# Row counts that are multiples of 16, and each expert's rows requested before the weight piece instead of behind it

## The chip, the cores and the metric

One Trainium2 chip, one of its cores. The metric is device time in microseconds (us) of one execution, lower is better. PE is the matrix engine, DVE the vector engine, ACT the scalar engine, POOL the GpSimd engine, SP the sync engine, which in this kernel only issues DMA transfers.

## The reference, cut to what matters

Three stages follow each other. A linear recurrence over 768 steps (4 batches, 8 heads, head size 48) gives 3072 rows of 384 numbers. A mixture of experts then picks one of 8 experts for each row; last comes a dense feed-forward layer. Only the middle stage is touched by the change:

```python
def _moe_ref(x, w_gate, w1, w2):          # x: 3072 x 384, w1: 8 x 384 x 1024, w2: 8 x 1024 x 384
    logits = x @ w_gate
    expert_idx = np.argmax(logits, axis=1)
    ...                                    # gate_w: the softmax probability of the chosen expert
    for e in range(E):
        mask = expert_idx == e
        xe = x[mask]
        h = np.maximum(xe @ w1[e], 0.0)
        ye = h @ w2[e]
        out[mask] = gate_w[mask, None] * ye

def _moe2_ref(x, w_in, w_out):            # 384 -> 2048 -> 384
    h = x @ w_in
    g = np.maximum(0.01 * h, h)
    return g @ w_out
```

## The kernel before, in words

**Stages.** Until about 150 us the kernel computes the recurrence, chooses an expert for each token and scatters the rows by expert into a DRAM table `xs` (8 regions; a row is 386 floats, 1544 bytes: 384 values, the gate weight, the token's number). From about 140 to 380 us the experts run, one after the other, sorted by how many tokens they got. From about 377 us to the end the dense layer runs over blocks of 512 tokens.

**Places and windows.** The experts stand in eight places; place k has room for `CAPS[k]` rows, fixed when the kernel is built, and the matmuls always run over the whole room. Place 0 is cut in two (256 and 224 rows), so there are nine windows, numbered 0 to 8; window i from 1 on serves place i - 1. Each window has eight steps f = 0 to 7, and n = 8 i + f counts all of them. A step issues `first(n)` (9 matmuls of 128 hidden units, tile `ph`; three products each, since every number is split into a high and a low part), then ACT and DVE make the hidden tile `hh` of it (L891, L892), and two steps later `second` uses it (9 matmuls, tile `y`, L911).

**Rows of a window.** `load_rows(i)` (L847) brings the rows of a window from `xs` into the tile `erows` with one DMA: the rows are cut into nj slices of w = cap / nj, slice after slice side by side on w partitions, so that the transfer runs over w partitions, then over nj rows on each. There is a single `erows` buffer. `turn(i)` (L863 to L867) transposes the rows on PE, one third of the columns at a time, in steps f = 2, 4 and 6 of the window before (5, 6 and 7 in window 1); ACT and DVE copy the result into `xe`. So `load_rows(i + 1)`, issued at f = 0 of window i, needs only that `turn(i)` has finished, which it did at f = 6 of the window before.

**Weights.** An expert's weights come in eight pieces of 384 KB. `piece_load(n + 2)` (L764) is issued by SP in step n into one of three `raw` buffers; it waits until `piece_split(n - 1)` is done: ACT copies the high half (L777), and for odd pieces POOL, for even ones DVE, makes the low half (L785). Pieces split in window i are used in window i + 1.

**Conversion.** In parallel `convert` turns the weights of the last layer from 64-bit numbers into 32-bit ones: SP loads `raw64` (L795), ACT makes `size` (L805), DVE does six operations (L815 to L835), and SP stores to `w2f` (L837).

**Orders.** Every engine runs its instructions in the order written, and so does SP's queue of transfers. At f = 0 of window i, with n = 8 i, SP's order before the change is: `piece_load(n + 2)`, then `load_rows(i + 1)`, then the `raw64` load and the `w2f` store. The loop that fixes this is `experts`:

```python
        for n, (i, f) in enumerate(seq):
            if n + AHEAD >= nf:
                self.piece_load(n + AHEAD)
            if n >= nf:
                if f == 0 and i + 1 < len(WINDOWS):
                    self.load_rows(i + 1, xs)
...
            if n >= nf:
                self.piece_split(n)
            self.convert_step(n, pools)
```

Of the kernel before, what the change touches and what calls it, by code (L numbers as in the profile page):

```python
# [21 lines left out]
P = 128  # L22
# [42 lines left out]
LISTS = 4  # L65
OUT_AT = (0, 1, 3, 5, 7, 9, 11, 13)

CAPS = (480, 456, 432, 416, 400, 392, 384, 372)
EARLY = 256
WINDOWS = [(0, 0, EARLY), (0, EARLY, CAPS[0] - EARLY)] + [(k, 0, CAPS[k]) for k in range(1, 8)]  # L70
PAD = 260
assert sum(CAPS) <= S * B + PAD

# [12 lines left out]
class Kernel:  # L86
# [110 lines left out]
    def cap_table(self):  # L197
        for k in range(E):
            self.nc.vector.memset(self.caps[:, k : k + 1], float(CAPS[k]))

# [114 lines left out]
    def load_start(self, k):  # L315
        SP, ACT = mybir.EngineType.SP, mybir.EngineType.Activation
        self.starts.append(self.index(self.starts_i[0:1, k : k + 1], NT + PAD - CAPS[k], [ACT, SP]))

# [27 lines left out]
    def attention(self, xs, clist, extra, first_weights, const, route):  # L346
        nc, tc, a = self.nc, self.tc, self.a
        with ExitStack() as ctx:
# [64 lines left out]
            def zero_region(e):  # L413

                n = max(CAPS) - SURE
                nc.sync.dma_start(
# [421 lines left out]
            del self.conv[i]  # L838


    def load_rows(self, i, xs, eng=None):

        k, off, cap = WINDOWS[i]
        nj = -(-cap // P)
        w = cap // nj
        self.win[i] = t = self.rowpool.tile([P, 4, RW], F32, tag="rows", name="erows")
        (eng or self.nc.sync).dma_start(  # L847
            out=t[:w, :nj, :],
            in_=xs[bass.ds(self.ids[k] * NT + off, cap), :].rearrange("(j p) c -> p j c", p=w),
        )  # L850

    def turn(self, i, ps, tag, cs=range(KD)):
        nc = self.nc
        k, off, cap = WINDOWS[i]
        nj = -(-cap // P)
        w = cap // nj
        for c in cs:
            if c == 0:
                self.xT[i] = self.xpool.tile([P, 2, KD, 512], F32R, tag="x", name="xe")
            x = self.xT[i]  # L860
            pt = ps.tile([P, 512], F32, tag=tag, name="pt") if ps else tag[c]
            for j in range(nj):
                nc.tensor.transpose(  # L863
                    pt[:, j * w : (j + 1) * w], self.win[i][:w, j, c * P : (c + 1) * P], self.ident[:w, :w]
                )
            nc.scalar.activation(out=x[:, 0, c, :cap], in_=pt[:, :cap], func=AF.Copy)
            nc.vector.tensor_tensor(  # L867
                out=x[:, 1, c, :cap], in0=pt[:, :cap], in1=x[:, 0, c, :cap].bitcast(F32), op=ALU.subtract
            )

    def list_rows(self, k, xs, clist):
        at = self.starts[k]
        self.nc.sync.dma_start(
            out=clist[bass.ds(at, CAPS[k]), :] if k else clist[0 : CAPS[0], :],
            in_=xs[bass.ds(self.ids[k] * NT, CAPS[k]), DM : DM + 2],
# [53 lines left out]
    def experts(self, xs, clist, pools, meanwhile):  # L929
        nf = FF // P  # L930
        seq = [(i, f) for i in range(len(WINDOWS)) for f in range(nf)]
        rest = iter(seq)

        self.starts = [0]

        self.sums(0, pools)

        def second(count):
            for _ in range(count):
                self.second(*next(rest), pools)  # L940

        for n, (i, f) in enumerate(seq):
            if n + AHEAD >= nf:
                self.piece_load(n + AHEAD)
            if n >= nf:
                if f == 0 and i + 1 < len(WINDOWS):
                    self.load_rows(i + 1, xs)
                if f == 6:
                    for k in {1: (1,), 2: (2, 3), 3: (4, 5), 4: (6, 7)}.get(i, ()):
                        self.load_start(k)  # L950

                if i >= 2 and f % LISTS == 1 and (n - 2 * nf) // LISTS < E:
                    self.list_rows((n - 2 * nf) // LISTS, xs, clist)
# [3 lines that stand above are left out]
            if n == nf:  # L957
                second(1)
            if n == 2 * nf:
                second(1)  # L960
            self.first(i, f, pools)
            meanwhile(n)

            second(2 if n == nf - 1 else 0 if nf <= n <= nf + 1 or n == 2 * nf else n >= LAG)
            if n == nf - 1:
                self.turn(1, pools["ps"], "h")

            turns = (5, 6, 7) if i == 1 else (2, 4, 6)
            if n >= nf and f in turns:
                if i + 1 < len(WINDOWS):  # L970
                    self.turn(i + 1, pools["ps"], "h", [turns.index(f)])
                else:
                    self.split_x(0, turns.index(f))
        self.rest = second
# [428 lines left out]
```

## Time and profile before

| | us |
|---|---|
| median of 3 runs | 795.03 (794.87 to 795.36) |
| the profiled execution | 792.69 |
| its span, first to last instruction | 791.1 |

In the profiled execution PE was busy 755.4 us of the span (95%), DVE 469.9, ACT 376.8, POOL 191.3; the mean granted clock of PE was 0.977 of full speed. The row of an instruction gives its start, how long it took, engine and line, tiles and shape; neighbours of one kind are merged (x9 is nine). A busy PE can be waiting inside its pipeline, so a stretch is better read from the starts of the groups than from the busy share.

### The profile page before, as it was taken

Reading aid. Unit: us, or ns where it says so; the run is one execution under the profiler, and the core shown is the slowest. Engines: PE = TensorE matmul, PEld = TensorE weight load, DVE = VectorE, ACT = ScalarE, POOL = GpSimd, SP = SyncE. Lnnn points to the kernel's source line nnn. Section 1 sums busy time; section 2 is a strip of 40 time slices with the busy share of each in tenths; the row PEclk is TensorE's granted clock in tenths of the full one; section 3 lists DMA queues with packets and bytes.
Section 4 is the critical chain, followed back from the end, with each engine's and each line's share of the span. In section 5 each row is a group of like instructions: output and inputs, shape, how many; then the busy total and the mean of one; then the engine's idle time right before and its main releaser. Section 6 shows DMA issues by size and latency. Waiting matters only on the chain.

```text
span 791.1 us, 13214 instructions
## 1 busy us (share of the span) xinstructions
PE 755.4 (95%) x4908; PEld 696.2 (88%) x4908; DVE 469.9 (59%) x837; ACT 376.8 (48%) x801; POOL 191.3 (24%) x214
## 2 busy tenths in 40 slices
PE   6999988999999999799999999999999999999994
PEld 3889977899999999799999899999999999999993
DVE  6878876568888999599874443433433343343331
ACT  5989976255555545355444423332342243233331
POOL 5768883402222232123100200020020001002001
PEclk8989999999999999899999999999999999999998
DMA  8899875468757757757530000010010001001001
GB/s 230 255 270 276 264 235 171 157 184 247 214 169 241 236 193 228 188 177 226 136 113 15 11 30 1 1 41 0 1 41 1 1 0 41 1 1 40 1 1 44
DMA packets 52373, 92.62 MB, mean 117 GB/s; under 512 B 12789, under 2 KB 30762, under 8 KB 52298
## 3 DMA queue, kind: packets, MB, share of 16 engines
q1 hardware_dynamic: 49017, 81.47, 34.8%
q0 software_dynamic: 3280, 10.21, 3.5%
q8 instruction: 40, 0.66, 0.4%
q14 instruction: 36, 0.29, 0.1%
HBM read 73.11 MB, written 18.57 MB: 116 GB/s over the span
## 4 chain that ended last, share of the span: by engine, by line
PE 66%; issue 8%; DMA 2%; DVE 2%; POOL 1%; ACT 0%; SPq 0%; POOLq 0%; ACTq 0%
PE ph L1005 21%; PE o L1024 21%; PE ph L886 12%; PE y L911 11%; DMA erows<-xs 2%; PE pt L863 1%; POOL out L1037 1%; DVE t L832 1%; POOL xs L742 0%; ACT z L1036 0%; DVE c L785 0%; POOL c L785 0%; DVE hh L892 0%; DVE t L823 0%; DVE t L829 0%
## 5 line engine op out<-in xcount | busy, mean ns | idle before, releaser
L1024 PE MATMUL o<-c,gg 128*128 128x384 f32 x1152 | 215.5, 336 | 0.0
L1005 PE MATMUL ph<-x,c 128*128 128x512 f32 x864 | 213.9, 392 | 0.0
L1024 PEld LDWEIGHTS o<-c,gg 128*128 128x128 f32 x1152 | 202.1, 188 | 8.2 <-DVE gg L1014 0.2
L1005 PEld LDWEIGHTS ph<-x,c 128*128 128x128 f32 x864 | 161.2, 188 | 28.5
L1011 DVE TENSOR_TENSOR s<-s,ph 128x512 f32<-128x512 f32 x96 | 65.9, 686 | 165.4 <-ACT s L1010 165.4
L1010 ACT ACTIVATE s<-ph 128x512 f32<-128x512 f32 x96 | 57.3, 597 | 174.0 <-PE ph L1005 165.0
L886 PE MATMUL ph<-xe,c 128*128 128x256 f32 (+8 forms) x648 | 126.8, 343 | 2.5 <-DVE xe L867 2.5
L911 PE MATMUL y<-hh,c 128*128 128x256 f32 (+8 forms) x648 | 122.0, 333 | 0.0
L886 PEld LDWEIGHTS ph<-xe,c 128*128 128x128 f32 x648 | 111.8, 196 | 4.6 <-DVE xe L867 2.6
L785 POOL TENSOR_TENSOR c<-raw,c 128x768 fp32r<-128x768 f32 x32 | 60.2, 1881 | 221.5 <-ACT c L777 150.5
L911 PEld LDWEIGHTS y<-hh,c 128*128 128x128 f32 x648 | 110.0, 190 | 2.1
L1014 DVE TENSOR_TENSOR gg<-s,gg 128x512 fp32r<-128x512 f32 x96 | 66.4, 692 | 67.0 <-ACT gg L1013 66.3
L1037 POOL DMA_INDIRECT out<-z,to x24 | 24.2, 1009 | 320.9 <-ACT z L1036 302.3
L1013 ACT ACTIVATE gg<-s 128x512 fp32r<-128x512 f32 x96 | 60.7, 632 | 81.2 <-DVE s L1011 81.2
L777 ACT ACTIVATE c<-raw 128x768 fp32r<-128x768 f32 x80 | 67.1, 840 | 3.6 <-DMA raw<-in_wE 2.9
L891 ACT ACTIVATE hh<-ph 128x256 fp32r<-128x256 f32 (+8 forms) x72 | 34.5, 479 | 71.2 <-PE ph L886 68.8
L471 ACT ACTIVATE A<-ident,av 128x128 f32<-128x128 f32 x192 | 58.6, 392 | 0.3 <-DVE av L461 0.2
L785 DVE TENSOR_TENSOR c<-raw,c 128x768 fp32r<-128x768 f32 x48 | 45.6, 951 | 11.3 <-ACT c L777 10.7
L832 DVE SCALAR_TENSOR_TENSOR t<-raw,t 128x384 f32<-128x384 uint32 x32 | 45.6, 1425 | 1.1
L892 DVE SCALAR_TENSOR_TENSOR hh<-ph,hh 128x256 fp32r<-128x256 f32 (+8 forms) x72 | 38.5, 535 | 8.3 <-ACT hh L891 8.3
L482 PE MATMUL pa<-R,K 48*128 48x128 f32 x384 | 29.7, 297 | 7.1 <-DVE A L488 5.3
L488 DVE COPY_PREDICATED A<-strict,pa 128x1024 f32<-128x1024 int32 x24 | 32.4, 1351 | 3.9 <-PE py L518 2.6
(175 smaller groups left out, 668.8 us busy)
## 6 DMA issues: line engine op xcount, KB each, us to landing
raw<-in_wE SPq DMA_DIRECT2D x64, 384.0 KB
raw<-in_w2nd SPq DMA_DIRECT2D x32, 384.0 KB
w2f<-t SPq DMA_DIRECT2D x32, 192.0 KB
raw<-w2f SPq DMA_DIRECT2D x16, 384.0 KB
k<-in_k SPq DMA_DIRECT2D x24, 192.0 KB
r<-in_r SPq DMA_DIRECT2D x24, 192.0 KB
v<-in_v SPq DMA_DIRECT2D x24, 192.0 KB
kT<-in_kT SPq DMA_DIRECT2D x40, 96.0 KB
```

What stands on the lines that cost most here:

```text
L471: nc.scalar.activation(out=d["A"][:, h % 2, h // 2, :], in_=self.ident, func=AF.Copy, scale=d["av"][:, h : h + 1],)
L777: self.nc.scalar.activation(out=w[:, 0, c], in_=t, func=AF.Copy)
L785: eng.tensor_tensor(out=w[:, 1, c], in0=t, in1=w[:, 0, c].bitcast(F32), op=ALU.subtract)
L832: nc.vector.scalar_tensor_tensor(out=x, in0=low.bitcast(U32), scalar=2.0**-52, in1=x, op0=ALU.mult, op1=ALU.mult)
L886: nc.tensor.matmul(ph[:, :cap], w[:, wl, c * 512 + o : c * 512 + o + P], self.xT[i][:, xl, c, :cap], start=(c == 0 and n == 0), stop=(c == ...
L911: nc.tensor.matmul(self.y[i][m][:, :cap], w[:, wl, o : o + P], t[:, xl, :cap], start=(f == 0 and n == 0), stop=(f == FF // P - 1 and n == 2),)
L1005: nc.tensor.matmul(ph, w[:, wl, c * 512 + off : c * 512 + off + P], x2[b][:, xl, c, :], start=(c == 0 and i == 0), stop=(c == KD - 1 and i ...
L1010: nc.scalar.activation(out=s, in_=ph, func=AF.Copy, scale=0.01)
L1011: nc.vector.tensor_tensor(out=s, in0=s, in1=ph, op=ALU.max)
L1013: nc.scalar.activation(out=t[:, 0, :], in_=s, func=AF.Copy)
L1014: nc.vector.tensor_tensor(out=t[:, 1, :], in0=s, in1=t[:, 0, :].bitcast(F32), op=ALU.subtract)
L1024: nc.tensor.matmul(o[b][k][:, :DM], t[:, gl, k * P : (k + 1) * P], w[:, wl, (f % 4) * DM : (f % 4 + 1) * DM], start=(f == 0 and i == 0), s ...
```

## The change

Two things. The rooms of places 1, 5 and 7 go from 456, 392 and 372 rows to 448, 400 and 368, so that each room is a multiple of 16; as 368 isn't divisible by 3, a new function `window` takes the smallest number of slices that divides the room (368 is four slices of 92 instead of 372 as three of 124). And from window 2 on `load_rows(i + 1)` is issued at the head of step f = 0, before `piece_load(n + 2)`; in window 1 it stays behind it.

```diff
-CAPS = (480, 456, 432, 416, 400, 392, 384, 372)
+CAPS = (480, 448, 432, 416, 400, 400, 384, 368)
...
+    def window(self, i):
+
+        k, off, cap = WINDOWS[i]
+        nj = next(n for n in range(-(-cap // P), 5) if cap % n == 0)
+        return k, off, cap, nj, cap // nj
+
     def load_rows(self, i, xs, eng=None):
 
-        k, off, cap = WINDOWS[i]
-        nj = -(-cap // P)
-        w = cap // nj
+        k, off, cap, nj, w = self.window(i)
...
     def turn(self, i, ps, tag, cs=range(KD)):
         nc = self.nc
-        k, off, cap = WINDOWS[i]
-        nj = -(-cap // P)
-        w = cap // nj
+        k, off, cap, nj, w = self.window(i)
...
         for n, (i, f) in enumerate(seq):
+
+            if i > 1 and f == 0 and i + 1 < len(WINDOWS):
+                self.load_rows(i + 1, xs)
             if n + AHEAD >= nf:
                 self.piece_load(n + AHEAD)
             if n >= nf:
-                if f == 0 and i + 1 < len(WINDOWS):
+                if i == 1 and f == 0:
                     self.load_rows(i + 1, xs)
```

## Rows read from the trace of the kernel before

**Rows 1.** Who waited for whom, engine PE, whole span: total, times, longest.

```profile
PE pt L863 <- DMA erows<-xs: 7.6, 2, 5.5
```

**Rows 2.** PE in order of time, windows 6 to 8.

```profile
315.78 0.49 PE L863 MATMUL pt<-ident,erows 128*128 128x128 f32 x3
...
327.30 1.74 PE L911 MATMUL y<-hh,c 128*128 128x384 f32 x9
334.54 0.88 PE L863 MATMUL pt<-ident,erows 124*128 124x124 f32 x3 [5.50 <-DMA erows<-xs]
...
339.58 1.75 PE L886 MATMUL ph<-xe,c 128*128 128x384 f32 x9
341.17 1.73 PE L911 MATMUL y<-hh,c 128*128 128x384 f32 x9
342.74 0.48 PE L863 MATMUL pt<-ident,erows 124*128 124x124 f32 x3
...
346.24 1.75 PE L886 MATMUL ph<-xe,c 128*128 128x384 f32 x9
...
360.62 1.69 PE L911 MATMUL y<-hh,c 128*128 128x372 f32 x9
```

**Rows 3.** The chain that ended last, 300 to 340 us: start, us, what.

```profile
317.70 1.83 POOL c L785
319.55 0.34 SPq L764
...
320.13 14.36 DMA erows<-xs
```

**Rows 4.** Stretches: length, busy PE, PEld, DVE, ACT, POOL; PE clock, DMA share, GB/s.

```profile
162.00:163.00 1.00, 1.00 (x7) 1.00 (x7) 0.31 (x1) 0.14 (x1) 0.00 (x0) 0.50 0.37 127
318.00:320.00 2.00, 2.00 (x13) 2.00 (x12) 1.97 (x2) 1.59 (x3) 1.52 (x1) 1.00 0.06 22
320.00:334.50 14.50, 9.04 (x52) 8.72 (x50) 7.96 (x12) 3.96 (x7) 1.85 (x1) 0.88 0.84 197
335.00:336.00 1.00, 1.00 (x6) 1.00 (x5) 0.01 (x1) 0.60 (x2) 0.00 (x0) 0.50 0.34 122
340.00:353.00 13.00, 13.00 (x78) 12.93 (x77) 12.72 (x21) 6.60 (x12) 3.66 (x2) 1.00 0.67 212
```

**Rows 5.** SP's queue in order of time: rows of windows 2, 7 and 8.

```profile
160.11 0.34 SPq L847 DMA_DIRECT2D erows<-xs  x1
...
293.21 0.40 SPq L847 DMA_DIRECT2D erows<-xs  x1
...
315.12 4.77 SPq L764 DMA_DIRECT2D raw<-in_wE  x2
320.13 0.28 SPq L847 DMA_DIRECT2D erows<-xs  x1
320.52 0.86 SPq L795 DMA_DIRECT2D raw<-in_w2nd  x1
```

**Rows 6.** PE in order of time: first use of the rows issued at 293.21.

```profile
302.21 0.49 PE L863 MATMUL pt<-ident,erows 128*128 128x128 f32 x3
```

**Rows 7.** ACT and DVE in order of time, windows 7 and 8.

```profile
326.31 0.84 ACT L777 ACTIVATE c<-raw 128x768 fp32r<-128x768 f32 x1
335.40 0.55 ACT L805 ACTIVATE size<-raw 128x384 f32<-128x384 f32 x1 [8.25 <-DMA raw<-in_w2nd]
327.18 0.96 DVE L785 TENSOR_TENSOR c<-raw,c 128x768 fp32r<-128x768 f32 x1
358.15 0.53 DVE L892 SCALAR_TENSOR_TENSOR hh<-ph,hh 128x372 fp32r<-128x372 f32 x1
```

**Rows 8.** Groups by line and shape, PE, 161 to 385 us: busy us, mean ns.

```profile
L911 PE MATMUL y<-hh,c 128*128 128x456 f32 x72 | 16.1, 368 | 0.0
L911 PE MATMUL y<-hh,c 128*128 128x432 f32 x72 | 15.5, 360 | 0.0
L911 PE MATMUL y<-hh,c 128*128 128x400 f32 x72 | 14.4, 344 | 0.0
L911 PE MATMUL y<-hh,c 128*128 128x392 f32 x72 | 14.3, 341 | 0.0
L911 PE MATMUL y<-hh,c 128*128 128x384 f32 x72 | 13.9, 337 | 0.0
L911 PE MATMUL y<-hh,c 128*128 128x372 f32 x72 | 13.3, 332 | 0.0
```

## The prediction

> **What bounds the kernel now.** I read the waits of PE first, since PE is busy for 95% of the span. Among them is one that the diff touches: the transposes wait for `erows` twice, 7.6 us together, 5.5 us the longer one [rows 1]. PE in order of time places the longer one in window 7, where the rows of window 8 (372 rows) are transposed for the first time [rows 2]; the shorter one belongs to the rows of window 1, which POOL requests, and the diff leaves that alone. Third, the chain that ended last says why window 8's rows came late: POOL makes the low half of a weight piece until 319.53, SP's `piece_load` waits for that, and only then does the request of the rows go out, at 320.13; it lands 14.36 us later [rows 3]. Last, the stretches tell what the transfer engines and DVE did meanwhile [rows 4].
>
> What that wait costs is more than 5.5 us. The `second` before it begins at 327.30; a group of the same shape in front of the next transposes takes 1.57 us from start to start (341.17 to 342.74), so the transposes were due at 328.87 and began at 334.54: 5.67 us late. Then PE ran at a granted clock of 0.50, its 1.2 GHz level: 335 to 336 us shows it, after PE had stood still for over 5 us [rows 4]. From the transposes' start to the start of the next `first` but one it took 5.04 us (334.54 to 339.58), against 3.50 undisturbed (342.74 to 346.24) [rows 2]: 1.54 us more. In all 7.21 us can be had here.
>
> **The order.** The rows of window 8 need their buffer free, which it is when the last transposes of window 7 end: 315.78 + 0.49 = 316.27 [rows 2]. SP has nothing left to do then but wait for POOL: of the two piece loads that begin at 315.12, one goes out there and the other at 315.12 + 4.77 - 0.33 = 319.56, behind POOL [rows 3, 5]. Put ahead of that second one, the request goes out at about 316.3, 3.8 us earlier. In 318 to 320 us the transfer engines were nearly idle (share 0.06), so it starts alone.
>
> **The size.** Is the transfer also faster? 372 rows in slices of 124 took 14.36 us [rows 3]. 384 rows in slices of 128, requested at the same place a window earlier, were there by their first use with no wait, 302.21 - 293.21 = 9.0 us later or sooner [rows 5, 6]. More bytes in less time: something about 372 or about 124 is slow. The load of window 2 (456 rows, slices of 114, requested at 160.11) tells which: at 162 to 163 us, before other loads come in, it holds 0.37 of the 16 transfer engines, 5.9 of them, at 127 GB/s [rows 4, 5]. 114 = 6 x 19 is cut evenly by 6; counted by the room, 456 = 8 x 57, one would expect 8 engines, a share of 0.50. So I take it that the number of partitions sets the spread. Then 124 = 4 x 31 ran on 4 engines, and 92 = 4 x 23 does so again: 368 being a multiple of 16 doesn't help, since the slices aren't.
>
> The Trainium skill speaks against the change here, in "DMA: Bandwidth & Descriptors", section "Why a DMA increments its semaphore by 16 and not by 1": the number of engines is the largest one up to 16 that divides the slowest dimension of both sides, which makes 6 of 114, 4 of 124, 4 of 92, and 10 of the 100 partitions that place 5 now has, for 14 before. The trace's 5.9 agrees with its 6. By this rule the sum is the one below; if the room itself were split, it would be that of the first rival.
>
> Transfer time of the 368 rows on 4 engines, both ends: alone, at 127 / 5.9 = 21.5 GB/s an engine, 368 x 1544 bytes = 568 KB need 6.6 us, with 2 us for start and landing (an estimate: window 2's load, requested at 160.11, moves from about 161 on) 8.6, so it lands at 324.9. Crowded all the way as before, 14.36 x 368 / 372 = 14.2, landing at 330.5. I take both in turn: alone from about 317.8 to 320.5 (232 KB), then at the crowded rate, 574 KB in 12.4 us = 46 GB/s, the other 336 KB in 7.3 us: landing at about 328.2. PE wants the rows at 328.87. So PE's direct wait goes to 0, with 0.7 us to spare; at the crowded end it would be 1.6.
>
> **What is late next.** The piece load that goes out at 319.56 (piece 58) now stands behind the rows on those 4 engines. How long it is held: the `raw64` load was requested 0.39 us behind the rows, and ACT could use it at 335.40, 0.9 us after the rows had landed [rows 3, 5, 7]. Piece 58 would so be there at about 329.2. ACT split it at 326.31, in order, so ACT stands still until then; ACT's half takes 0.84, and DVE, which made the low half at 327.18, makes it at 330.1 or so: 3 us late. Behind it in DVE's order stand the conversion, `hh` and the `xe` of window 8. DVE can't catch up: it is busy for 12.72 of 13 us in 340 to 353 [rows 4]. The nearest use is the `hh` of step 0 of window 8: DVE finishes it at 358.15 + 0.53 = 358.68, and PE begins with it at 360.62 [rows 2, 7], 1.94 us to spare. So I put back 3.0 - 1.94 = 1.0 us of waiting; between 0, if the rows land at 327 or earlier, and 2, if they land at 329.
>
> In windows 2 to 6 the rows also go out about 3.5 us earlier, ahead of a piece that ACT splits some 7 us after it was requested (319.56 and 326.31 in window 7, [rows 5, 7]); a load on 10 to 16 engines (100, 104, 108 or 128 partitions) has landed long before. I count nothing, covered by that distance. In window 2 the piece is itself 0.6 us later, since SP has the rows to request first; the same cover. The 400 rows of place 5 on 10 engines may take a few us more; 9.0 us was enough for 384 rows, and they go out earlier: nothing. The 448 rows of place 1, in slices of 112 = 7 x 16, come faster; nothing waited on PE for them: nothing.
>
> **The columns.** Each place has 72 matmuls in `second` and as many in `first`, where I take the same times, as window 7's `first` holds the stall. 456 to 448: (16.1 - 15.5) x 8 / 24 = 0.20 us; 392 to 400: 0.1 more; 372 to 368: (13.9 - 13.3) x 4 / 12 = 0.20 [rows 8]. Twice that sum, 0.3, is 0.6 us less; with tenths rounded I take 0.4. Place 7 has 12 transposes for 9, but of 92 columns: up to 0.1 us. The instructions on DVE and ACT shrink or grow by 2% and lie beside PE.
>
> **The sum.** 5.67 + 1.54 + 0.4 - 0.1 - 1.0 = 6.5 us less. The profiled execution took 792.69 us (1.6 of them outside its span), so 786.2 by its own time; the runs' median is 795.03, 2.3 above it, and from there I predict 788.5 us.
>
> **The rivals.** (1) The whole room counts after all: 368 rows spread over 16 engines. For it: 384 rows were quick. Against it: the 0.37. Then the rows land before 325.3 (316.3 + 9.0), piece 58 isn't held, and the 1.0 isn't put back: 787.5.
> (2) The load is crowded from the start and lands at 330.5: PE waits 1.6 us, the clock takes up to 1.5 again, and DVE, 5 us late by the same steps, less the 3.1 that PE itself is late, asks for nothing beyond: 7.2 + 0.3 - 3.1 = 4.4 less, 790.6. For it: 320 to 334.5 ran at 197 GB/s at a share of 0.84, where much was queued. Against: the idle 318 to 320.
> (3) No change: the stall moves to the pieces. If everything behind the rows comes so late that DVE loses about 9 us instead of 3, PE gets 7 of it: 795. It takes a landing of piece 58 at 335, 18 us after the request of the rows; the slowest one seen is 14.36.
> (4) Slower: DVE's lack of idle time. Each of the six windows from 2 on now puts its rows ahead of a piece; if each piece came later than its use and cost DVE time that it can't regain, the first 1.94 us are covered and all else is paid by PE. From (7.5 + 1.9) / 6 = 1.6 us a window on, the gain is gone; at 2 us a window it would be 797.6. Against it: the 7 us between request and use.
> That a room is too small, so that the slow path for leftovers runs, is out: with the default seed the reference gives the experts 410, 409, 403, 389, 380, 374, 359 and 348 rows.
>
> **Chances.** The forecast 0.57 (787.6 to 789.8 by its own bounds for what is put back), rival 1 0.15, rival 2 0.16, rival 3 0.07, rival 4 0.05. A measurement of this kernel can tell about 0.2% (1.6 us) from no change. Faster by more than that are the first three, 0.88; within it 0.07; slower 0.05. The range of 8 in 10 goes from 786.8, below rival 1 by what the columns and the unprofiled runs leave open, to 792.8, between rivals 2 and 3.
>
> **What would show it.** Right: the request of window 8's rows goes out about 3 us before POOL ends the low half, its transposes follow `second` with no wait worth naming and no 1.2 GHz stretch after 320 us; ACT stands still for some 2 to 3 us in front of piece 58; small waits of PE for `hh` or `xe` early in window 8. Wrong on the size: ACT doesn't wait there, and the DMA share right after the request is far above 0.25 (4 of 16). Wrong altogether: PE's wait is there with another releaser, or ACT waits for pieces in windows 2 to 6 too.

## The result, and the profile after

The changed kernel's median is 785.83 us of 3 runs (784.52 to 788.2), before it was 795.03: ratio 0.9888, 95% interval 0.9850 to 0.9926, 9.2 us less. In a second comparison it was 786.99 against 794.14: 0.9902 (0.9875 to 0.9929), 7.2 us less. The forecast was 788.5 with a range from 786.8, so the first result lies below the range.

PE in order of time, changed kernel, the rows that answer to [rows 2] (the first matmuls of windows 2, 7 and 8 and of the dense layer, the first transposes of window 8's rows, the first use of window 8's hidden units):

```profile
177.35 3.85 PE L889 MATMUL ph<-xe,c 128*128 128x448 f32 x18
...
317.83 1.73 PE L889 MATMUL ph<-xe,c 128*128 128x384 f32 x9
...
325.83 1.74 PE L914 MATMUL y<-hh,c 128*128 128x384 f32 x9
327.40 0.48 PE L866 MATMUL pt<-ident,erows 92*128 92x92 f32 x4
...
344.20 1.69 PE L889 MATMUL ph<-xe,c 128*128 128x368 f32 x9
...
351.91 1.68 PE L914 MATMUL y<-hh,c 128*128 128x368 f32 x9
...
368.63 2.21 PE L1011 MATMUL ph<-x,c 128*128 128x512 f32 x9
```

The first matmuls of windows 2, 7 and 8 and of the dense layer in the kernel before:

```profile
178.85 3.92 PE L886 MATMUL ph<-xe,c 128*128 128x456 f32 x18
...
319.35 1.75 PE L886 MATMUL ph<-xe,c 128*128 128x384 f32 x9
...
352.87 1.69 PE L886 MATMUL ph<-xe,c 128*128 128x372 f32 x9
...
377.48 2.25 PE L1005 MATMUL ph<-x,c 128*128 128x512 f32 x9
```

The transposes of window 8 start 1.57 us after the `second` in front of them, as undisturbed ones do; the 5.5 us wait is gone. SP's queue in order of time, changed kernel, answering to [rows 5]:

```profile
314.73 0.29 SPq L852 DMA_DIRECT2D erows<-xs  x1
317.97 0.35 SPq L765 DMA_DIRECT2D raw<-in_wE  x1
```

The rows are requested at the moment when their buffer is free (window 7's last transposes end at 314.21 + 0.49 = 314.70) and 3.2 us ahead of piece 58. Stretches of the changed kernel (columns as in [rows 4]): the first while the rows alone are moving, then one that answers to [rows 4]:

```profile
317.50:319.00 1.50, 1.50 (x10) 1.50 (x9) 1.47 (x3) 0.56 (x2) 0.44 (x1) 1.00 0.26 99
320.00:334.50 14.50, 14.50 (x88) 14.43 (x87) 12.51 (x21) 7.97 (x15) 3.70 (x2) 1.00 0.83 236
```

A share of 0.26 is 4 of 16 engines: 92 partitions are spread no wider than 124 were. PE's granted clock stays at 1.00 after 320 us. The 448 rows of window 2 in slices of 112 now fill 0.92 of the engines at 162 to 163 us, where the 456 rows in slices of 114 held 0.37.

ACT, DVE and POOL, changed kernel, answering to [rows 7]: piece 58 is late, and the `hh` of step 0 of window 8 is ready at 349.87 + 0.54 = 350.41, 1.50 us before PE takes it up at 351.91:

```profile
326.44 0.85 ACT L778 ACTIVATE c<-raw 128x768 fp32r<-128x768 f32 x1 [1.48 <-DMA raw<-in_wE]
327.32 0.96 DVE L786 TENSOR_TENSOR c<-raw,c 128x768 fp32r<-128x768 f32 x1 [1.72 <-ACT c L778]
329.79 1.86 POOL L786 TENSOR_TENSOR c<-raw,c 128x768 fp32r<-128x768 f32 x1 [6.99 <-ACT c L778]
330.37 1.50 DVE L830 TENSOR_SCALAR t<-t 128x384 int32<-128x384 int32 x1
349.87 0.54 DVE L895 SCALAR_TENSOR_TENSOR hh<-ph,hh 128x368 fp32r<-128x368 f32 x1
```

**Where the time went.** Three cuts of the span, from the starts of the same groups:

| | before | after |
|---|---|---|
| start to window 2's first matmuls | 178.85 | 177.35 |
| from there to the dense layer's first (the stretch that the change touches) | 198.63 | 191.28 |
| the rest of the span | 413.6 | 414.3 |

So 7.35 us of the span's 8.2 come from where they were looked for. The 1.5 us in front aren't the change's: no request is moved there, and the one room that is loaded there, 448 rows for 456, isn't it either, since the run below with the old rooms began window 2 at 177.40. That start differs from run to run. I use the middle stretch as the measure, because it repeats: 198.63 and 199.31 in two profiles of the kernel before, 191.28 and 191.25 in two of the changed one.

### The profile page after: what moved, and what is told of

Same layout as the page of the kernel before. It is cut to its first block, busy times and chain, and to the rows that moved or that the text cites. A ratio compares the mean times of both kernels' runs of the same rounds, so it can differ in the third digit from the quotient of the medians.

```text
span 782.9 us, 13219 instructions
## 1 busy us (share of the span) xinstructions
PE 754.6 (96%) x4911; PEld 695.2 (89%) x4911; DVE 468.5 (60%) x837; ACT 377.7 (48%) x801; POOL 191.4 (24%) x214
## 4 chain that ended last, share of the span: by engine, by line
PE 86%; POOL 4%; DMA 3%; ACT 2%; DVE 2%; issue 1%; SPq 1%; POOLq 0%; DVEq 0%; ACTq 0%
PE o L1030 25%; PE ph L1011 25%; PE ph L889 14%; PE y L914 14%; PE py L519 2%; DMA r<-in_r 2%; PE pa L483 2%; PE py L513 1%; ACT A L472 1%; PE pr L558 1%; PE pt L866 1%; POOL rk L449 1%; POOL rk L448 1%; DMA erows<-xs 1%; DVE A L489 1%
## 5 line engine op out<-in xcount | busy, mean ns | idle before, releaser
L889 PE MATMUL ph<-xe,c 128*128 128x400 f32 (+7 forms) x648 | 124.3, 338 | 2.5 <-DVE xe L870 2.5
L914 PE MATMUL y<-hh,c 128*128 128x400 f32 (+7 forms) x648 | 121.4, 332 | 0.0
L889 PEld LDWEIGHTS ph<-xe,c 128*128 128x128 f32 x648 | 109.4, 192 | 4.3 <-DVE xe L870 2.6
L786 POOL TENSOR_TENSOR c<-raw,c 128x768 fp32r<-128x768 f32 x32 | 60.3, 1885 | 213.9 <-ACT c L778 167.6
L894 ACT ACTIVATE hh<-ph 128x400 fp32r<-128x400 f32 (+7 forms) x72 | 34.5, 479 | 68.5 <-PE ph L889 66.1
L786 DVE TENSOR_TENSOR c<-raw,c 128x768 fp32r<-128x768 f32 x48 | 45.6, 952 | 13.8 <-ACT c L778 13.3
L833 DVE SCALAR_TENSOR_TENSOR t<-raw,t 128x384 f32<-128x384 uint32 x32 | 44.0, 1376 | 1.1
L895 DVE SCALAR_TENSOR_TENSOR hh<-ph,hh 128x400 fp32r<-128x400 f32 (+7 forms) x72 | 38.5, 535 | 7.1 <-ACT hh L894 7.1
```

What stands on the lines that cost most here:

```text
L786: eng.tensor_tensor(out=w[:, 1, c], in0=t, in1=w[:, 0, c].bitcast(F32), op=ALU.subtract)
L889: nc.tensor.matmul(ph[:, :cap], w[:, wl, c * 512 + o : c * 512 + o + P], self.xT[i][:, xl, c, :cap], start=(c == 0 and n == 0), stop=(c == ...
L914: nc.tensor.matmul(self.y[i][m][:, :cap], w[:, wl, o : o + P], t[:, xl, :cap], start=(f == 0 and n == 0), stop=(f == FF // P - 1 and n == 2),)
```

## The experiments

Theory A was the prediction's: the number of partitions of a slice sets the number of transfer engines, 92 gets 4 as 124 did, and the earlier request does the work. Theory B was the reading behind the change: a room that is a multiple of 16 makes the load quick. What each run gave, with medians of the same chip beside it:

| run | median, before | ratio (95%) | stretch | PE's wait in window 7 |
|---|---|---|---|---|
| order alone | 789.48, 794.14 | 0.9947 (0.9930 to 0.9965) | 191.96 | none |
| rooms alone | 789.84, 794.14 | 0.9953 (0.9934 to 0.9972) | 195.94 | 2.9 |
| rooms, last one 360, old order | 784.18, 794.14 | 0.9882 (0.9854 to 0.9910) | 190.75 | none |
| changed kernel again | 786.99, 794.14 | 0.9902 (0.9875 to 0.9929) | 191.25 | none |
| loads split, new order | 783.31, 792.12 | 0.9887 (0.9856 to 0.9917) | 191.28 | none |
| loads split, old order | 783.38, 792.12 | 0.9886 (0.9855 to 0.9916) | 191.28 | none |
| last room 376, new order | 792.64, 792.12 | 0.9995 (0.9971 to 1.0018) | 198.18 | 4.7 |
| before again | 793.65, 792.12 | 1.0012 (0.9993 to 1.0030) | 199.31 | 5.6 |
| only window 8's rows first | single run, 792.84 | | 191.28 | none |
| last room 368 alone, old order | single run, 793.47 | | 196.05 | 3.1 |
| last room 348, old order | single run, 793.38 | | 196.54 | 3.7 |

In the single runs the whole time can't be compared: the third from last row has the changed kernel's stretch to 0.01 us, but its window 2 began at 186.04, 8.7 us later than in the changed kernel's first profile, with nothing changed upstream. Over the 13 profiles that start lay between 175.70 and 186.04.

**Order alone.** The kernel before with only the order changed:

```diff
-CAPS = (480, 448, 432, 416, 400, 400, 384, 368)
+CAPS = (480, 456, 432, 416, 400, 392, 384, 372)
```

> Rooms as in the kernel before (456, 392, 372), only the order changed: the rows are requested ahead of the piece from window 2 on. Theory A (the spread goes by the slice's partitions, so the room sizes do nothing for the last load, and the earlier request does it all): window 8's rows, 372 in slices of 124, still on 4 engines, are requested near 316 and land before PE asks; no PE wait in window 7; time within 0.6 us of the changed kernel's, some 8 us under before. Theory B (the room counts, a multiple of 16 makes the load quick): 372 isn't one, the load stays at 14 us and lands near 330, PE waits 1 to 2 us and its clock falls: 3 to 5 us under before.

No wait for the rows, so theory B's landing at 330 is out; 372 rows on 4 engines are quick enough if they start early. But it isn't the changed kernel's time: the median is 2.5 us above it on the same chip, with 0.7 us more in the stretch and then a wait of PE that the changed kernel doesn't have. PE, ACT and DVE of this run:

```profile
345.78 0.61 PE L889 MATMUL ph<-xe,c 128*128 128x372 f32 x2 [0.26 <-DVE xe L870]
...
371.80 0.73 PE L1011 MATMUL ph<-x,c 128*128 128x512 f32 x2 [0.65 <-DVE x L988]
327.41 0.85 ACT L778 ACTIVATE c<-raw 128x768 fp32r<-128x768 f32 x1 [2.48 <-DMA raw<-in_wE]
328.29 0.96 DVE L786 TENSOR_TENSOR c<-raw,c 128x768 fp32r<-128x768 f32 x1 [2.63 <-ACT c L778]
```

Here the held piece costs DVE 2.63 us instead of 1.72, and PE pays twice. In the first step of window 8 `xe` is late: that group takes 2.06 us from start to start (344.17 to 346.23) where the next takes 1.53 (347.81 to 349.34), 0.53 us more, and the old rooms' columns (0.2 between before and after) account for the rest of the 0.7. The chain that ended last in 315 to 376 us leads to this wait from the piece's load (requested at 318.07, 9.26 us), over ACT's copy and DVE's instructions in order. At the dense layer's first matmuls `x` is late as well, and the group after it starts at 372.37, 3.01 us after 369.36, against 2.05 in the changed kernel (368.63 to 370.68), 0.96 us; how much of that is the piece's isn't shown. So the prediction's mechanism exists, early in window 8 as it said, but only when the piece is held longer than in the changed kernel.

**Rooms alone.** The changed kernel with the old order:

```diff
-            if i > 1 and f == 0 and i + 1 < len(WINDOWS):
-                self.load_rows(i + 1, xs)
...
-                if i == 1 and f == 0:
+                if f == 0 and i + 1 < len(WINDOWS):
                     self.load_rows(i + 1, xs)
```

> Rooms as changed (448, 400, 368), the order as before. Theory A: 368 rows in slices of 92 run on 4 engines as 372 in slices of 124 did, land some 14 us after a request near 320, and PE waits 5 us and more: within 1.5 us of before. Theory B: the load is spread over 16 engines, lands within 9 us, no PE wait: 7 to 8 us under before.

Neither. The chain of this run:

```profile
320.68 11.85 DMA erows<-xs
```

PE still waits for the rows, 2.9 us, as theory A has it, but the load took 11.85 us where it had been 14.36. From window 7 to window 8 that is worth 2.5 us (33.52 to 31.03); with 0.2 us of columns the stretch is 2.7 us shorter (198.63 to 195.94), and the median 4.3 us, more than the stretch accounts for.

**The spread, three times over.** First 360 rows, which is no multiple of 16, in slices of 120 = 8 x 15, in the old order (that part of the edit is as above):

```diff
-CAPS = (480, 448, 432, 416, 400, 400, 384, 368)
+CAPS = (480, 448, 432, 416, 400, 400, 384, 360)
```

> As the run with the rooms alone and the old order, but the last place has 360 rows, not a multiple of 16, in 3 slices of 120 = 8 x 15 partitions. Theory A: 15 engines, the rows land within 9 us, no PE wait in window 7: 7 to 9 us under before with the old order. Theory B: 360 = 8 x 45 isn't a multiple of 16, slow load, PE waits: within 2 us of before.

Theory A, at 10 us under before rather than 7 to 9. The rows were requested at 323.06 and used at 331.91 without a wait, 8.9 us later, in the old order. Its stretch is another 0.53 us shorter than the changed kernel's: 8 columns fewer in 144 matmuls. Second, 376 rows in slices of 94 = 2 x 47, in the new order:

```diff
-CAPS = (480, 448, 432, 416, 400, 400, 384, 368)
+CAPS = (480, 448, 432, 416, 400, 392, 384, 376)
```

> The changed order, but the last place has 376 rows in 4 slices of 94 = 2 x 47 (and place 5 its old 392). Theory A: 2 engines; alone they would need 13 us and more, so the rows land at 331 or later although requested near 316; PE waits 2 us or more, its clock falls, ACT and DVE wait for the held pieces: 4 to 12 us slower than the changed kernel, near or above before. Theory B (the room counts): 376 = 8 x 47, 8 engines, quicker than 4: no PE wait, at or below the changed kernel.

A stretch while its rows alone were moving, then its chain:

```profile
321.00:322.00 1.00, 1.00 (x8) 1.00 (x7) 0.96 (x2) 0.47 (x2) 0.40 (x1) 1.00 0.13 46
```

```profile
318.18 17.44 DMA erows<-xs
```

A share of 0.13 is 2 of 16 engines; the load took 17.44 us although it went out as soon as its buffer was free, PE waited 4.7 us for it, and all of the gain was lost (0.9995). Third, the changed kernel's own 368 rows, cut by partitions into two transfers:

```diff
-        (eng or self.nc.sync).dma_start(
-            out=t[:w, :nj, :],
-            in_=xs[bass.ds(self.ids[k] * NT + off, cap), :].rearrange("(j p) c -> p j c", p=w),
-        )
+        src = xs[bass.ds(self.ids[k] * NT + off, cap), :].rearrange("(j p) c -> p j c", p=w)
+        even = w // 16 * 16
+        for lo, hi in ((0, even), (even, w)):
+            if lo < hi:
+                (eng or self.nc.sync).dma_start(out=t[lo:hi, :nj, :], in_=src[lo:hi])
```

> The changed kernel, but each load of a window's rows is cut into two DMAs by partitions: the largest multiple of 16 (80 of 92 for the last), and the rest (12). Same rows, same bytes, same order. Theory A (the spread goes by the slice's partitions, and a load on 4 engines holds up the pieces behind it, which costs ACT and DVE time that PE pays in part): window 8's rows are there within 9 us of their request, ACT no longer waits for the piece behind them, PE never waits in windows 7 and 8; 2 to 3 us under the changed kernel, beside the run with 360 rows (784.2). Theory C (what the 360-row run gained over the changed kernel is its fewer columns and chance, the held piece is hidden): within 1 us of the changed kernel's 787.0.

ACT no longer waits for the piece, yet the stretch is 191.28, the changed kernel's own. So in the changed kernel the held piece costs PE nothing in the stretch: theory C on this point, and my expectation of 2 to 3 us from it was wrong. The median beside the changed kernel's (0.9887 and 0.9902, intervals overlapping) tells nothing more. The same split with the old order:

> The same split loads with the order as before (rows behind the piece). Theory A: once the load is on 12 to 16 engines the order is worth nothing; same time as the split in the new order within 1 us, 9 to 10 us under before. Theory D (the earlier request is needed as well): PE waits for window 8's rows, 2 us or more slower than the split in the new order.

191.28 again and 0.9886: with the loads spread, it doesn't matter whether the rows or the piece go first. Each half of the cure is enough to end the wait, a load spread over 12 or more engines or an early request of a load on 4 (on 2 it wasn't); this split and the 360-row room also leave the pieces free.

**Controls.** The changed kernel and the kernel before, once more:

> The changed kernel again, beside the others on one chip: 7 to 10 us under before. In its profile the 1.2 GHz stretch near 160 us, after PE's wait for window 1's rows, may be there or not: nothing that the change touches lies ahead of it; if it comes and goes between runs of one kernel it is chance, worth some 1.7 us.

The 1.2 GHz stretch after PE's wait for window 1's rows was in the profile before (162 to 163 us, a clock of 0.50, [rows 4]), not in the changed kernel's first profile (1.00 there, after a wait of 1.76 us), and again in this one (0.57 at 162 to 164 us, after a wait of 2.7 us). It is chance, as far as the change goes.

> The kernel before, once more, for a second trace of it. If its 14.4 us for 372 rows in slices of 124 is its rule, the load takes 13 to 15 us here too and PE waits 5 us or more in window 7; if part of it was chance, it is nearer the 9 to 10 us from first to last packet that the 368 rows took with the rooms changed alone, and the wait is nearer 3 us. Time as before, within 0.2%.

The load took 14.43 us here, after 14.36: its rule, not chance.

Only window 8's rows moved ahead, the others behind the piece as before (`if i == 7` for `if i > 1`):

> Rooms as changed; only window 8's rows are requested ahead of the piece, those of windows 3 to 7 behind it as before. If the earlier requests of the other windows do nothing (the prediction's claim), the stretch of PE from window 2's first matmul to the dense layer's first is that of the changed kernel, 191.3 us, within 0.2; if they help or hold up pieces, it is off by more.

191.28: the moves in windows 2 to 6 do nothing.

The last room alone 368, all else as before:

> Order as before and rooms as before, but the last is 368 in 4 slices of 92. The run with all new rooms and the old order landed its 368 rows 11.85 us after the request, against 14.4 for 372 rows in 3 slices of 124, both on 4 engines. If the last room's slicing makes that difference, 11.5 to 12.2 us here and 2.5 to 3.2 us of waiting; if the other rooms do (448, 400), 14 us and 5 us of waiting.

It is the last room's slicing: 11.95 us, a wait of 3.1. And 348 rows in three slices of 116 = 4 x 29:

> Order as before, new rooms, the last one 348 rows in 3 slices of 116 = 4 x 29 (348 is what the smallest expert gets): 4 engines, 87 rows each. If three slices against four is what made 372 slower than 368, the 116-partition load runs at the pace of the 124-partition one: 12.4 x 87 / 93 + 2 = 13.6 us to landing, PE waits 4 us or more. If the row count alone sets it, at the 368 rows' pace: 9.85 x 87 / 92 + 2 = 11.3 us, and PE waits 2 to 3 us.

12.70 us, between the two expectations. With 92, 87 and 93 rows an engine (slices of 92, 116 and 124) the loads took 11.9, 12.7 and 14.4 us; that 116 ran on 4 engines is taken from the division, its share wasn't seen alone. Neither the row count nor three slices against four explains that; the order is that of the partitions, but what sets the pace stays open.

## Why the prediction was wrong, point by point

- **What bounds the kernel.** Right. 7.21 us were said to be had in window 7; from the first matmuls of window 7 to those of window 8 it went from 33.52 to 26.37 us, 7.15 less.
- **The order.** Right: requested when the buffer came free, 3.2 us before POOL's end was past.
- **The size.** Right on the spread: 4 engines for 92 partitions as for 124 (0.26 alone in both the changed kernel and the order-alone run, 0.13 for 94). The section of the Trainium skill's "DMA: Bandwidth & Descriptors" that the prediction weighed ("Why a DMA increments its semaphore by 16 and not by 1") gives 2 for 94 and 4 for 124 and 92; the shares agree. Wrong in that the new slicing was said not to help: on the same 4 engines it takes 2.5 us off the load in the old order (14.36 to 11.85), where my crowded end took off 0.2. What makes it quicker stays open.
- **What is late next: the term that failed.** The 1.0 us put back wasn't there. Piece 58 was to come 9.6 us after its request (319.56 to 329.2) and to hold DVE up by 3.0 us; it came 8.5 us after (317.97 to 326.44) and DVE waited 1.72. And "DVE can't catch up" was wrong: of these 1.72, at step 0 of window 8 only 1.94 - 1.50 = 0.44 were left. The split run in the new order, whose piece isn't held, has 1.91 us to spare there; the changed kernel's second profile and the run with only window 8's rows first, where DVE waited 2.03 and 2.33, have 1.51 and 1.50 and no wait of PE in windows 7 and 8. It took the 9.3 us and 2.63 of the order-alone run for PE to pay, 0.53 us in window 8. DVE's busy share of 98% in [rows 4] isn't all work: in the changed kernel L833 (L832 before) takes 0.56 us by itself (at 331.90) and 2.24 when POOL's L786 runs beside it (at 316.12), 1.7 more. Behind the held piece that overlap fell on L830, 1.50 us for 0.35, 1.15 more, and once more in the next such pair (1.52): twice some 0.5 us won back. A share made of such waits has room in it.
- **The columns.** 0.4 was expected, with 0.1 back for the transposes. Window 2 to window 7 was 140.50 before and 140.48 after (448 for 456 against 400 for 392); window 8 to the dense layer 24.61 and 24.43. So 0.2.
- **The sum.** The stretch gained 7.35 where 6.5 was forecast: 0.85 us too little, mostly the 1.0. That would have given 787.7 from the same base, inside the range.
- **The range.** The other 1.9 us of the miss to 785.83 lie outside the stretch, in the base and in the chance of three runs a side; the forecast gain of 6.5 us, a ratio of 0.9918, lies inside both measured intervals. I laid the saving on a median of three runs, knowing that it stood 2.3 us above the profiled execution. Later runs of the kernel before spread from 788.72 to 797.33, while its touched stretch differed by 0.7 us between two profiles; the start of window 2 moves by chance by more than that. The low end, 0.7 us below rival 1, left no room for it.
- **The rivals.** Rival 1's mechanism (16 engines) didn't happen; its time was the nearest by luck, as it put nothing back. Rival 2 didn't come for 368 rows; a load that lands after PE asks for it is what the 376-row run shows, at 17.4 us in place of 14.2. Rivals 3 and 4 didn't come: windows 2 to 6 neither gained nor lost.

## What to carry to other kernels

Look at how many of the 16 transfer engines hold a load while nothing else is moving: the share tells it, and the slice's partition count, not its row total, decides it (0.13 for 94 partitions, 0.26 for 92 and 124, 0.92 for 112); choose slices that 16 divides, or nearly, as 120, or cut the odd remainder off as a transfer of its own. A load that is thin (on few engines) and can't be widened goes out as soon as its buffer is free, ahead of what waits for other engines. Measure such a change on the stretch that it touches, between starts of the same instructions: there it repeated to 0.03 us in the changed kernel, where whole runs spread over several.

## What I had not expected of the hardware

Loads on 4 engines differ in pace beyond their rows: 11.85 and 11.95 us for 368 rows on 92 partitions, 14.36 and 14.43 for 372 on 124, at the same place in the queue and with 92 and 93 rows an engine. Why isn't shown. And a DVE instruction beside a POOL tensor operation can take 2.2 us for 0.56, so that a DVE that was busy for 21.52 of 22 us (328 to 350, changed kernel) still made up 1.3 us in some 23.
